# A searched program order, copies split by item, and a first token mix in halves, in a fused chunk-attention and wave-MLP kernel

## Chip, cores, metric

One core of a Trainium2 chip. The metric is the device time of one execution in microseconds (us), the median of several; lower is better. The profiled span of an execution is shorter than the time counted for the same execution (226.9 against 228.72 before the change).

## The reference

Chunked attention (chunks of 64 tokens, 8 heads of 64), then a layer that mixes tokens and channels:

```python
scores = 1/8 * (q_c @ k_c^T);  attn = softmax(scores);  x = attn @ v_c      # per 64-token chunk
theta = x @ w_theta
y = w_tok_r @ (x*cos(theta)) + w_tok_i @ (x*sin(theta))                      # over 576 tokens
u = x + y
out = u + relu(u @ w_ch)
```

The batch of 8 is worked in 4 pairs. 576 tokens of two batches are 9 blocks of 128, in five groups g = 0..4 of 2, 2, 1, 2, 2 blocks; group 2 is the block shared by both batches ("mid"). So a name such as a1 of (2,0) means step a1, pair 2, group 0.

## The kernel before

The engines are PE (TensorE, the matmuls; transposes run on it too), DVE (VectorE), ACT (ScalarE) and POOL (GpSimd). PSUM is the memory that PE writes its results to. Each pair goes through small steps. All use PE and one of four PSUM buffers, which DVE or ACT empties:

```python
a1(p,g)  # 32 transposes of q, k; qT copied by DVE, kT by ACT
a2(p,g)  # scores, exp on ACT
a3(p,g,hg)  # attn @ v; reciprocal and product on DVE
a4(p,g)  # transpose x; copy xT by ACT.  For the mid group:
        nc.scalar.copy(out=xm, in_=psv)
        for bb in range(2):
            nc.gpsimd.tensor_copy(                       # POOL
                out=xT[:, :, bb * S + KT * P : (bb + 1) * S],
                in_=xm[:, :, bb * CH : bb * CH + CH],
            )
a5(p,g)  # theta; cos and sin on ACT;  z(p,g): x*cos, x*sin on DVE
y(p,bb,db)  # token mix, 18 matmuls; uT = ps_y + xT on DVE
w(p,j)   # u @ w_ch and u; relu on ACT, sum and store (st)
```

The order comes from a small planner that weaves the attention of the next pair between the token mixes of this one. Loads cast f32 to f16 and are issued by POOL, the whole next pair at once:

```python
    for p in range(NP):
        ...                                    # first half of pair p, a4 of its mid group in it
        if more:
            new_pair(p + 1)
            load_batch(p + 1, B0 + B1)         # five groups: q, k, v
        ...                                    # second half, with a1, a2 of pair p+1 woven in
```

The softmax here doesn't subtract the row's maximum and nothing guards it: scores larger than these inputs give would overflow.

## Time and profile before

| | before |
|---|---|
| median time, us | 231.42 (229.97 to 231.69, 4 runs) |
| profiled span, us | 226.9 |
| PE busy | 89% |
| ACT, DVE busy | 58%, 53% |

Where a row of 40 digits is shown, it cuts the span into 40 equal slices, and each digit is the busy share of one slice in tenths. In a timeline a line has the start, the length, the engine, the source line, the operation, out<-in, the shape, and in brackets how long the engine had been idle and what ended it. The page's chain that ended last, by engine:

```profile
PE 75%; ACT 14%; DVE 6%; DMA 2%; issue 1%; POOL 0%; DVEq 0%; ACTq 0%; POOLq 0%
```

Three quarters of it are PE, so the way to less time is to fill PE's gaps. The view of stretches (start:end, length, then busy us of PE, PEld (weight loads), DVE, ACT, POOL; then the granted clock of PE, the DMA share and GB/s) shows how much there is:

```profile
110.00:170.00 60.00, 56.52 (x966) 40.46 (x961) 33.52 (x60) 39.99 (x45) 21.16 (x28) 1.00 0.84 104
170.00:222.00 52.00, 50.37 (x510) 33.41 (x508) 30.09 (x51) 24.19 (x33) 1.50 (x2) 1.00 0.20 64
```

PE lacks 3.5 us in 60 and 1.6 in 52: some 5 us in 112.

### The profile page before, as it was taken

The numbers are of one execution on the slowest core, as the hardware profiler recorded it, in microseconds if no ns is written. First come the engines' busy times: TensorE is split into PE (matmuls) and PEld (weight loads), VectorE is DVE, ScalarE is ACT, GpSimd is POOL, SyncE is SP. The second block draws the span as 40 slices with busy tenths as digits, with TensorE's granted clock in tenths as the row PEclk, the third lists the DMA queues.
The fourth block names the chain that finished last, engine by engine and source line by source line (L and its number), as shares of the span: only waits on it lengthen the run. The fifth ranks groups of instructions, "written<-read, shape, count | busy, mean of one in ns | idle before, by whom it ended". The sixth has DMA issues, their size and how long they took to land.

```text
span 226.9 us, 6743 instructions
## 1 busy us (share of the span) xinstructions
PE 201.7 (89%) x2994; PEld 140.3 (62%) x2994; DVE 120.2 (53%) x214; ACT 130.5 (58%) x151; POOL 88.5 (39%) x124
## 2 busy tenths in 40 slices
PE   0678979997898998999898998999898998999992
PEld 0564567855676656766785656666785657667751
DVE  0135373825547478446446477446456477356353
ACT  2355968357885881167785880267785880364142
POOL 8995487499100195981000295971000200000000
PEclk9999999999999999999999999999999999999998
DMA  6999999999920179999400189999200124013036
GB/s 63 165 156 186 192 180 187 144 124 168 222 22 3 48 102 197 221 168 208 129 3 3 49 118 225 195 169 222 99 3 3 49 69 139 3 46 139 2 110 217
DMA packets 83581, 26.93 MB, mean 119 GB/s; under 512 B 76256, under 2 KB 78944, under 8 KB 83552
## 3 DMA queue, kind: packets, MB, share of 16 engines
q0 software_dynamic: 77664, 16.54, 82.3%
q1 hardware_dynamic: 5888, 9.96, 12.6%
q8 instruction: 23, 0.38, 0.7%
q14 instruction: 6, 0.05, 0.1%
HBM read 33.06 MB, written 9.44 MB: 187 GB/s over the span
## 4 chain that ended last, share of the span: by engine, by line
PE 75%; ACT 14%; DVE 6%; DMA 2%; issue 1%; POOL 0%; DVEq 0%; ACTq 0%; POOLq 0%
PE ps_y L476 32%; PE ps_uw L496 13%; PE ps_theta L420 13%; ACT eT L342 5%; PE ps_qkT L307 5%; PE ps_sT L335 3%; PE ps_uw L503 3%; DMA qk<-in_k_dram 2%; PE ps_xT L391 2%; DVE uT L484 2%; DVE x L377 2%; ACT kT L317 2%; ACT cos L430 2%; ACT xT L398 2%; PE ps_x L363 2%
## 5 line engine op out<-in xcount | busy, mean ns | idle before, releaser
L476 PE MATMUL ps_y<-wT,z 128*128 128x288 f16 x512 | 68.2, 286 | 4.5 <-DVE x L377 2.4
L476 PEld LDWEIGHTS <-z 128*128 128x128 f16 x512 | 48.6, 98 | 18.5 <-DVE x L377 2.7
L246 POOL DMA_DIRECT2D v<-in_v_dram x56 | 42.1, 776 | 14.6 <-DMA qk<-in_k_dram 9.2
L484 DVE TENSOR_TENSOR uT<-ps_y,xT 128x576 f16<-128x576 f32 x32 | 24.2, 758 | 40.0 <-PE ps_y L476 40.0
L496 PE MATMUL ps_uw<-wch,uT 128*128 128x512 f16 x144 | 41.0, 379 | 2.3 <-ACT xT L398 1.7
L317 ACT COPY kT<-ps_qkT 128x1024 f16<-128x1024 f16 (+1 forms) x20 | 23.4, 1193 | 17.9 <-DVE qT L316 17.9
L404 POOL COPY xT<-xTm 128x256 f16<-128x256 f16 x8 | 4.9, 652 | 72.3 <-ACT xTm L402 72.3
L420 PE MATMUL ps_theta<-wtheta,xT 128*128 128x512 f16 x128 | 31.2, 388 | 1.7 <-ACT xT L398 1.7
L430 ACT ACTIVATE cos<-ps_theta,pihalf 128x1024 f16<-128x1024 f32 (+1 forms) x20 | 20.6, 1030 | 19.8 <-PE ps_theta L420 19.8
L503 PE MATMUL ps_uw<-id,uT 128*128 128x128 f16 x144 | 31.5, 219 | 0.0
L509 ACT ACTIVATE relu<-ps_uw 128x512 f32<-128x512 f32 x36 | 20.8, 603 | 18.4 <-PE ps_uw L503 18.4
L398 ACT COPY xT<-ps_xT 128x1024 f16<-128x1024 f16 x16 | 16.2, 1012 | 23.0 <-PE ps_xT L391 23.0
L515 DVE TENSOR_TENSOR o<-ps_uw,relu 128x512 f32<-128x512 f32 x36 | 24.0, 687 | 7.3 <-ACT relu L509 7.3
L307 PE MATMUL ps_qkT<-id,qk 128*64 128x128 f16 (+1 forms) x640 | 22.1, 227 | 6.4 <-DMA qk<-in_q_dram 5.8
L377 DVE TENSOR_TENSOR x<-ps_x,recip 128x512 f16<-128x512 f32 x36 | 24.9, 692 | 1.2
L307 PEld LDWEIGHTS <-qk 128*64 128x64 f16 (+1 forms) x640 | 18.9, 118 | 9.4 <-DMA qk<-in_q_dram 6.2
L316 DVE COPY qT<-ps_qkT 128x1024 f16<-128x1024 f16 (+1 forms) x20 | 12.6, 636 | 22.7 <-PE ps_qkT L307 22.7
L496 PEld LDWEIGHTS <-uT 128*128 128x128 f16 x144 | 14.1, 98 | 15.8
L420 PEld LDWEIGHTS <-xT 128*128 128x128 f16 x128 | 12.6, 100 | 15.7 <-ACT xT L398 2.1
L342 ACT ACTIVATE eT<-ps_sT 128x1024 f16<-128x1024 f32 (+1 forms) x20 | 18.3, 939 | 7.1 <-PE ps_sT L335 7.0
L443 DVE TENSOR_TENSOR z<-x,cos 128x1024 f16<-128x1024 f16 x16 | 11.1, 691 | 20.6 <-ACT cos L430 20.4
L225 POOL DMA_DIRECT2D qk<-in_k_dram x24 | 19.2, 804 | 3.6 <-DMA wch<-in_moe_w_ch_dram 1.6
(41 smaller groups left out, 199.1 us busy)
## 6 DMA issues: line engine op xcount, KB each, us to landing
out_dram<-o SPq DMA_DIRECT2D x32, 256.0 KB, 3.9
qk<-in_q_dram POOLq DMA_DIRECT2D x16, 256.0 KB, 6.4
qk<-in_k_dram POOLq DMA_DIRECT2D x16, 256.0 KB, 7.4
v<-in_v_dram POOLq DMA_DIRECT2D x40, 64.0 KB, 6.7
v<-in_v_dram POOLq DMA_DIRECT2D x16, 128.0 KB, 6.6
out_dram<-o SPq DMA_DIRECT2D x8, 128.0 KB, 4.1
wnat<-in_moe_w_tok_r_dram POOLq DMA_DIRECT2D x1, 576.0 KB, 9.9
wnat<-in_moe_w_tok_i_dram POOLq DMA_DIRECT2D x1, 576.0 KB, 11.9
```

The lines of the kernel that those rows point to most:

```text
L246: nc.gpsimd.dma_start(v16[pp : pp + m, sl, :, 0:D], v[2 * p + bb, :, s0 : s0 + m, :].rearrange("h s d -> s h d"),)
L307: nc.tensor.transpose(psv[par * D : par * D + D, w, e, tk, 0:rows], t[0:rows, w, 2 * e + par, tk, :], id16[0:rows, 0:rows],)
L317: nc.scalar.copy(out=kT[:, :, 0:rows, :].rearrange("p e s t -> p e t s"), in_=psv[:, 1, :, :, 0:rows],)
L342: nc.scalar.activation(out=eT[:, 0:n].rearrange("p i e r c -> p r (i e) c"), in_=psv[:, :, 0:n].rearrange("p r i e c -> p r (i e) c"), fun ...
L377: nc.vector.tensor_tensor(out=xo, in0=px[:, :, :, 0:D], in1=recip.broadcast_to((P, 2, NE, D)), op=ALU.mult,)
L420: nc.tensor.matmul(ps[:, jj * DM : jj * DM + DM], xt[:, db, :], wtheta16[:, db, :], start=(db == 0), stop=(db == NDB - 1),)
L430: nc.scalar.activation(out=cos[:, 0:n].rearrange("p a e -> p (a e)"), in_=pin, func=AF.Sin, bias=pihalf, scale=1.0,)
L476: nc.tensor.matmul(psv[:, hf, 0:HS], z[:, db * P : db * P + P], wT[:, kt, hf * HS : hf * HS + HS], start=(kt == 0), stop=(kt == 2 * KT),)
L484: nc.vector.tensor_tensor(out=s["uT"][:, db, sl].rearrange("p (f c) -> p f c", f=2), in0=psv[:, :, 0:HS], in1=s["xT"][:, db, sl].rearrange ...
L496: nc.tensor.matmul(ps[:, 0:DM], uT[:, db, j * P : j * P + P], wch16[:, db, :], start=(db == 0), stop=(db == NDB - 1),)
L503: nc.tensor.matmul(ps[:, DM + db * P : DM + db * P + P], uT[:, db, j * P : j * P + P], id16,)
L515: nc.vector.tensor_tensor(out=o, in0=ps[:, DM : 2 * DM], in1=r, op=ALU.add)
```

## The change

Its intent: replace the planner by a fixed list of items, found by annealing on a model of the engines; let each item say which engine makes its copies (the digit after the colon); begin the first token mix of pair 0 when half of the token weights are there. Loads run up to seven groups ahead, and each is issued as soon as the item that frees its buffer stands in the list. The core of the diff, cut:

```diff
+ORDER = """
+a1.0.0:3 a1.0.1:2 a2.0.0:0 a1.0.2:1 a3.0.0.0:0 a3.0.0.1:0 a2.0.1:0 a3.0.1.0:0 a2.0.2:0
+a3.0.2.0:0 a4.0.0:0 a4.0.2:1 ...
+... tw.1.1:1 yh.0.0:0 a1.0.3:3 yh.0.1:0 a2.0.3:0 a1.0.4:2 yh.1.0:0 a2.0.4:0 a3.0.3.0:0
+a1.1.2:3 yh.1.1:0 a2.1.2:0 a3.0.4.0:0 a1.2.0:0 a3.0.3.1:0 a1.1.0:0 a3.0.4.1:0 a2.2.0:0
+w.0.0:0 ...
-        nc.vector.tensor_copy(out=qT[:, :, :, 0:rows], in_=psv[:, 0, :, :, 0:rows])
-        nc.scalar.copy(out=kT..., in_=psv[:, 1, :, :, 0:rows])
+        copy(not bits & 1, qT[:, :, :, 0:rows], psv[:, 0, :, :, 0:rows])   # true: DVE, else ACT
+        copy(bits & 2, kT..., psv[:, 1, :, :, 0:rows])
...
+    LOADS = [(p, g) for p in range(NP) for g in BATCH[0] + BATCH[1]]
...                                        # the first seven loads up front, then:
+    for item in ORDER:
+        emit[kind](*args)
+        seen.add(name)
+        while loaded < len(LOADS):
+            p, g = LOADS[loaded]
+            pn, gn = LOADS[loaded - NAT]               # NAT = 7
+            need = {f"a1.{pn}.{gn}"}
+            if p >= 2:
+                need |= {f"a3.{p - 2}.{g}.{hg}" for hg in range(GROUPS[g][1])}
+            if not need <= seen:
+                break
+            load(loaded)
+            loaded += 1
```

## The prediction

> **What bounds the kernel now.** I read the page first (engine shares, the 40 slices, the issues of loads), then the timelines of PE, POOL, DVE and ACT over the first 70 us, then the waits.
>
> Engine shares and slices of the page:
> ```profile
> PE 201.7 (89%) x2994; PEld 140.3 (62%) x2994; DVE 120.2 (53%) x214; ACT 130.5 (58%) x151; POOL 88.5 (39%) x124
> ...
> POOL 8995487499100195981000295971000200000000
> ...
> DMA  6999999999920179999400189999200124013036
> ```
> PE is the bound: 89% busy, no other engine above 58%. POOL computes next to nothing; it is busy because it issues the loads of q, k, v. For the first eleven slices (62 us) it is near full and the DMA row is full: the weights and the first two pairs of batches stream in.
>
> The POOL timeline:
> ```profile
> 31.81 0.76 POOL L258 DMA_DIRECT2D wch<-in_moe_w_ch_dram  x1
> 32.56 0.75 POOL L404 COPY xT<-xTm 128x256 f16<-128x256 f16 x2
> 33.24 0.89 POOL L225 DMA_DIRECT2D qk<-in_q_dram  x1
> ...
> 54.82 1.47 POOL L246 DMA_DIRECT2D v<-in_v_dram  x2
> 56.48 0.89 POOL L246 DMA_DIRECT2D v<-in_v_dram  x1 [0.18 <-issue]
> 78.73 1.20 POOL L404 COPY xT<-xTm 128x256 f16<-128x256 f16 x2 [21.37 <-ACT xTm L402]
> ```
> POOL works strictly in order. At 31.81 it issues w_ch, at 32.56 it makes the two small copies xT<-xTm of pair 0, from 33.24 to 57.37 it issues the 25 loads of pair 1, and then it stands at the next copy for 21.37 us although loads stand behind it. So 25 issues take 24.1 us here: some 0.58 to 0.97 us each, plus about 5 us in which an issue waited for an earlier DMA.
>
> The issues of the page:
> ```profile
> qk<-in_q_dram POOLq DMA_DIRECT2D x16, 256.0 KB, 6.4
> qk<-in_k_dram POOLq DMA_DIRECT2D x16, 256.0 KB, 7.4
> ```
> A q or k load lands 6.4 and 7.4 us (median) after its issue.
>
> The DVE timeline, the first sum uT of pair 0:
> ```profile
> 35.98 0.76 DVE L484 TENSOR_TENSOR uT<-ps_y,xT 128x576 f16<-128x576 f32 x1 [1.68 <-PE ps_y L476]
> ```
> It reads xT, the middle columns that POOL copies included. The copy ended at 33.3, so this sum waited for PE alone. This is the place to remember.
>
> The waits of PE after 66 us sum to only 6.3 us in the trace, and PE is without a gap from 190 to 222. What a better order can win lies there and in the start.
>
> **What the Trainium skill says.** (1) "Perfetto Trace Analysis", section "DMA Instruction — SWDGE (GPSIMD)": the end shown for such a DMA is the end of descriptor generation, not of the transfer. The trace agrees: 0.6 to 1.0 us on POOL against 6.4 to 7.4 us to landing. (2) "ScalarE: Activation LUTs", "What ACT_TABLE_LOAD costs": about 1283 ns a load. The trace has 1283 ns, ten times. (3) "VectorE: DVE Perf Modes", the perf-mode tier table: a copy that reads PSUM runs at 2x at most. The trace agrees as far as it goes: the 1024-element copy qT takes 0.69 us on DVE, and xT, of the same size, 1.01 us on ACT. (4) "TensorE: Matmul & The Clock Gate", "What's actually happening": after an idle window PE starts at half clock. The trace shows it in
> ```profile
> 21.38 2.85 PE L420 MATMUL ps_theta<-wtheta,xT 128*128 128x512 f16 x8
> 24.94 1.89 PE L420 MATMUL ps_theta<-wtheta,xT 128*128 128x512 f16 x8
> ```
> where the same eight theta matmuls take 2.85 us early and 1.89 us later; the slices' clock row shows nothing of it.
>
> **The change part by part.** PE's work is the same: 5990 PE instructions in both built programs. I price each item by the length of its stretch in the PE timeline, without waits: a1 (32 transposes) 1.02 us, 0.66 for the half-size group; a2 0.63 and 0.35; a3 0.26; a4 0.45 and 0.22; a5 0.865 a token block; y 2.22; w 1.09; wT transposes 3 in all. With 36 w, 32 y and so on this gives 192.3 us. (PE's 201.7 is larger because each stretch also counts its draining tail.) Against 226.9 us there are 34.6 us to win: 5.8 before q lands, about 4.3 after the last matmul, 12.6 in the start up to 33.5 us (where 15.1 of the 192.3 are done), 2.4 from there to 66 (45.2 done), and about 9 after it.
>
> *Copies by item.* DVE takes 11 of the 20 xT copies (11 x about 0.95 leaves ACT, 11 x about 0.6 comes to DVE); qT and kT are exchanged in part (9 kT to DVE, 11 qT to ACT), about even. Two of ten table loads go: 2.6 us. ACT becomes about 117 us, DVE about 128. Neither bounds, so this counts only as smaller gaps.
>
> *First token mix in halves.* Four items of 18 matmuls, 256 or 320 columns wide in place of 288: same PE time. It could begin before the second half of the token weights is there. In the order, though, all six wT items stand before it, so it wins one or two us of the start at most.
>
> *New order and early loads.* Here I part with the intent. The loads now run seven groups ahead, issued as soon as a1 of an older group stands in the program. a1 of groups (0,0), (0,1), (0,2) are the first items, so loads (1,2), (1,3), (1,4) go into POOL's stream before the copy xT<-xTm of pair 0. The built program says so: that copy is POOL row 67, after all loads of pair 1; the kernel before has it ahead of all of these. POOL therefore reaches it only after the 25 issues that ended at 57.4 us, less the 0.7 us that the copy took ahead of them: about **57 us**, done about 58.3. The DVE instruction for the third half-mix (yh.1.0) waits for that copy, and DVE is in order. PE reaches yh.1.0 at about 38 us. With four PSUM buffers PE can run three items further, to about 43, and stands until 59.
>
> Next, the order puts a1 of group (2,0) seventh after yh.1.0, ahead of every w. Its load is POOL's next after the copy: q issued by 59.2, k by 60.1, and landing 6 us later, as the DMA still has pair 1 to finish (it fell idle at 63 in the kernel before): about 65.5. PE ends this a1 at **66.5 us**. By then it has done 28.8 us of its 192.3; the kernel before had done the 45.2. **The stall puts it 16.4 us behind.**
>
> What is left: 192.3 - 28.8 = 163.5 us, so the last matmul can't end before 230.0. Add 1.5 us for the half clock after the long pause (the theta line above lost 0.96 in one group), 5 us of gaps (before had about 9 in 147; I give the annealing half of it), and 4.3 for the last relu, sum and store. The span becomes 66.5 + 163.5 + 1.5 + 5 + 4.3 = **240.8 us**. The timed runs lie 3.1 to 4.8 us above the profiled span before; I add 3.7: **244.5 us**.
>
> Later loads hold nothing up by the same arithmetic: (2,1) is issued by 66.5 and used near 77, (3,1) issued by 90 and used near 105; POOL's copy for pair 1 falls near 93 and its first y sum near 107.
>
> **The rivals.** *The order works as meant.* If loads of (2,0) and the copy came by 45 us, PE would end near 192.3 + 5.8 + 4.3 plus 10 of gaps, 212 us of span, 216 timed, 7% faster. For it: PE's work is unchanged and gaps are to be had; an order found on a calibrated model should respect arrivals. Against it: POOL's stream before 57 us is full from end to end, and the same 9.4 MB precede this load in both kernels. *The stall is there but short.* If POOL issues faster (0.75 us each with no waits for DMAs, copy at 52) and the load lands in 4.5 us, PE passes at 60; with 3 us of gaps the span is 60 + 163.5 + 1.5 + 3 + 4.3 = 232.3 and the time 236: within 2%. For it: the shortest landing in the trace is 3.4 us. Against it: DMA is full in these slices. *ACT or DVE bind after the stall.* Between a1 of (2,0) and the next theta, 14 us of PE work carry about 11 us of ACT and 12 of DVE; with four PSUM buffers gaps could be 10 us rather than 5: 250 us.
>
> **Range and chances.** The copy's time is good to 1.5 us, landing to 2, gaps to 4: together 5 us at one in ten. Range 236.5 to 251. Faster by over 2% needs the whole stall to be absent: 0.04. Within 2% needs 8 us less: 0.09. Slower: 0.87.
>
> **What would show it.** In the new profile: POOL's copy xT<-xTm near 57 us with issues just ahead; a DVE wait of over 12 us for POOL at the half-mix sum; PE slices near zero from about 43 to 66 us, the last of it ended by DMA of k; PE busy nearly whole after it; eight table loads; ACT near 117 and DVE near 128. If the copy comes before 45 us, or PE has no gap over 5 us between 40 and 66, the argument is wrong.

## The result

| | before | after |
|---|---|---|
| median time, us | 231.42 | 246.12 (244.7 to 247.11, 4 runs) |
| ratio of fast runs | 1 | 1.0644 (95%: 1.0571 to 1.0717) |
| profiled span, us | 226.9 | 242.7 |

The kernel became 6.4% slower. A ratio here is the mean time of one kernel's fast runs over that of the other's in the same rounds, so it is not quite the ratio of the medians quoted. Executions over 1.5% slower than the fastest of the same kernel are left out of the means.

The page after, shares and slices:

```profile
PE 203.8 (84%) x2994; PEld 142.0 (58%) x2994; DVE 128.4 (53%) x223; ACT 117.3 (48%) x137; POOL 88.8 (37%) x126
...
PE   0849996063298999958999999999999999999992
...
POOL 8994686799779777940000200000010000000000
PEclk9999999557579999997999999999999999999998
DMA  7999999999999999993104021201321212221236
```

PE has a hole in slices 7 to 11, at 40 to 67 us. The clock row falls to 5 with it. DMA is full up to the eighteenth slice; loads now stream without a break. The chain that ended last:

```profile
PE 66%; DMA 16%; POOL 9%; issue 3%; DVE 2%; ACT 2%; ACTq 0%; POOLq 0%
```

DMA was 2% of it and POOL 0%; now they are 16% and 9%. POOL's timeline:

```profile
55.14 2.32 POOL L177 DMA_DIRECT2D v<-in_v_dram  x3
57.37 0.83 POOL L362 COPY xT<-xTm 128x256 f16<-128x256 f16 x2
58.05 0.96 POOL L156 DMA_DIRECT2D qk<-in_q_dram  x1
58.92 0.96 POOL L156 DMA_DIRECT2D qk<-in_k_dram  x1
...
97.09 0.76 POOL L362 COPY xT<-xTm 128x256 f16<-128x256 f16 x2
```

The mid copy of pair 0 stands at 57.37, after all loads of pair 1, and q and k of (2,0) follow it. In the kernel before it stood at 32.56. DVE:

```profile
37.81 1.30 DVE L198 COPY kT<-ps_qkT 128x1024 f16<-128x1024 f16 x1
57.90 0.82 DVE L443 TENSOR_TENSOR uT<-ps_y,xT 128x640 f16<-128x640 f32 x1 [18.78 <-POOL xT L362]
```

Between these two lines DVE did nothing for 18.78 us: the half-mix sum reads the columns that POOL copies. PE over the hole:

```profile
37.10 1.26 PE L435 MATMUL ps_y<-wT,z 128*128 128x320 f16 x8
...
40.16 0.30 PE L321 MATMUL ps_x<-v,eT 64*64 64x65 f16 x16
50.41 1.37 PE L267 MATMUL ps_qkT<-id,qk 64*64 64x64 f16 x32 [9.95 <-DMA qk<-in_q_dram]
51.72 2.31 PE L435 MATMUL ps_y<-wT,z 128*128 128x320 f16 x8
...
60.25 0.46 PE L293 MATMUL ps_sT<-qT,kT 64*64 64x64 f16 x16 [3.66 <-DVE kT L198]
...
63.76 1.06 PE L267 MATMUL ps_qkT<-id,qk 128*64 128x128 f16 x16 [2.83 <-DMA qk<-in_q_dram]
66.81 1.06 PE L267 MATMUL ps_qkT<-id,qk 128*64 128x128 f16 x16 [1.99 <-DMA qk<-in_k_dram]
```

Three waits lie in a row: 9.95 us for q of group (1,2), 3.66 for DVE's copy kT, which stood behind the wait for POOL, and 2.83 + 1.99 for q and k of (2,0). After them the order does what it was made for (stretches, as above):

```profile
70.00:110.00 40.00, 34.81 (x797) 24.91 (x798) 28.83 (x52) 30.38 (x32) 30.29 (x41) 1.00 1.79 166
110.00:170.00 60.00, 60.00 (x931) 42.57 (x932) 35.99 (x64) 34.16 (x42) 1.50 (x2) 0.97 0.14 44
170.00:230.00 60.00, 60.00 (x509) 40.02 (x507) 33.21 (x55) 26.33 (x35) 0.75 (x2) 1.00 0.22 73
```

From 110 us PE is busy 120 us of 120, where the kernel before lost 5 of 112. So the search did fill the gaps; the hole ahead of them cost more.

### The profile page after: what moved, and what is told of

It reads as the page before. It is cut to its first block, busy times and chain, and to the rows that moved or that the text cites. A ratio compares the mean times of both kernels' runs of the same rounds, so it can differ in the third digit from the quotient of the medians.

```text
span 242.7 us, 6736 instructions
## 1 busy us (share of the span) xinstructions
PE 203.8 (84%) x2994; PEld 142.0 (58%) x2994; DVE 128.4 (53%) x223; ACT 117.3 (48%) x137; POOL 88.8 (37%) x126
## 4 chain that ended last, share of the span: by engine, by line
PE 66%; DMA 16%; POOL 9%; issue 3%; DVE 2%; ACT 2%; ACTq 0%; POOLq 0%
PE ps_y L456 26%; DMA qk<-in_k_dram 12%; PE ps_uw L476 12%; PE ps_theta L378 11%; PE ps_qkT L267 5%; POOL v L177 4%; DMA wnat<-in_moe_w_tok_r_dram 4%; POOL qk L156 3%; PE ps_uw L483 3%; PE ps_xT L349 3%; PE ps_sT L293 3%; PE ps_x L321 2%; ACT kT L200 1%; DVE qT L198 1%; DVE o L495 1%
## 5 line engine op out<-in xcount | busy, mean ns | idle before, releaser
L456 PE MATMUL ps_y<-wT,z 128*128 128x288 f16 x448 | 60.7, 290 | 0.0
L456 PEld LDWEIGHTS <-z 128*128 128x128 f16 x448 | 42.8, 99 | 13.2
L267 PE MATMUL ps_qkT<-id,qk 128*64 128x128 f16 (+1 forms) x640 | 24.7, 238 | 21.8 <-DMA qk<-in_q_dram 18.9
L476 PE MATMUL ps_uw<-wch,uT 128*128 128x512 f16 x144 | 42.5, 379 | 0.2 <-ACT kT L200 0.2
L464 DVE TENSOR_TENSOR uT<-ps_y,xT 128x576 f16<-128x576 f32 x28 | 21.2, 756 | 32.4 <-PE ps_y L456 32.2
L267 PEld LDWEIGHTS <-qk 128*64 128x64 f16 (+1 forms) x640 | 20.8, 125 | 24.5 <-DMA qk<-in_q_dram 19.6
L156 POOL DMA_DIRECT2D qk<-in_q_dram x24 | 19.4, 811 | 1.0 <-POOLq L559 0.8
L200 ACT COPY qT<-ps_qkT 128x1024 f16<-128x1024 f16 (+1 forms) x11 | 9.5, 859 | 20.6 <-PE ps_qkT L267 20.5
L200 ACT COPY kT<-ps_qkT 128x1024 f16<-128x1024 f16 (+1 forms) x11 | 13.3, 1212 | 11.7 <-DVE qT L198 11.7
L392 ACT ACTIVATE sin<-ps_theta 128x1024 f16<-128x1024 f32 (+1 forms) x20 | 18.7, 937 | 0.0
```

The lines of the kernel that those rows point to most:

```text
L156: nc.gpsimd.dma_start(t[(pp // 2) : (pp // 2) + m // 2, ti].rearrange("p h t d -> p h (t d)"), src.rearrange("h (p t) d -> p h (t d)", t=2),)
L200: nc.scalar.copy(out=out, in_=in_)
L267: nc.tensor.transpose(psv[par * D : par * D + D, w, e, tk, 0:rows], t[0:rows, w, 2 * e + par, tk, :], id16[0:rows, 0:rows],)
L456: nc.tensor.matmul(psv[:, hf, 0:HS], zt[:, db * P : db * P + P], wT[:, kt, hf * HS : hf * HS + HS], start=(kt == 0), stop=(kt == 2 * KT),)
L464: nc.vector.tensor_tensor(out=uT_tile(p)[:, db, sl].rearrange("p (f c) -> p f c", f=2), in0=psv[:, :, 0:HS], in1=xT_tile(p)[:, db, sl].rea ...
L476: nc.tensor.matmul(ps[:, 0:DM], uT[:, db, j * P : j * P + P], wch16[:, db, :], start=(db == 0), stop=(db == NDB - 1),)
```

## The experiments

Twelve kernels ran. The question was which of the two late arrivals made the hole, POOL's copy or the loads, and whether the order and the split are good once they are fed. The first four ran on one chip, the next four on another; each is compared with the kernel before. Kernels are compared only within the same rounds.

### 1. The mid copy on DVE

```diff
-            nc.gpsimd.tensor_copy(
+            nc.vector.tensor_copy(
```

> Edit: in the changed kernel the two small copies xT<-xTm go to DVE instead of POOL; order and loads stay. Main theory (two late arrivals in series: POOL's copy, and the loads of groups (1,2) and (2,0) which the order uses before they land): DVE's 18.8 us wait for POOL is gone, but PE still waits near 40 for q of (1,2) until about 50 and for k of (2,0) until about 66; time 244 to 247 us, the same as the changed kernel. Rival A (the copy behind the loads is the cause): the stall is gone, 228 to 231 us. Rival B (the new order or the new split of copies is slow by itself): 246 us, with PE gaps elsewhere.

Measured 244.48 us, ratio 1.058 (1.0523 to 1.0637). PE's timeline:

```profile
50.67 1.34 PE L267 MATMUL ps_qkT<-id,qk 64*64 64x64 f16 x32 [9.77 <-DMA qk<-in_q_dram]
...
64.51 1.06 PE L267 MATMUL ps_qkT<-id,qk 128*64 128x128 f16 x16 [7.01 <-DMA qk<-in_q_dram]
66.20 1.06 PE L267 MATMUL ps_qkT<-id,qk 128*64 128x128 f16 x16 [0.63 <-DMA qk<-in_k_dram]
```

The wait for POOL is gone and the time is not: PE waits for the same two groups until nearly the same moments (50.67 and 66.20, against 50.41 and 66.81). Rival A falls: the copy by itself is not worth 15 us.

### 2. The copy on DVE, the early items later

```diff
-a2.0.4:0 a3.0.3.0:0 a1.1.2:3 yh.1.1:0 a2.1.2:0 a3.0.4.0:0 a1.2.0:0 a3.0.3.1:0 a1.1.0:0 a3.0.4.1:0 a2.2.0:0
+a2.0.4:0 a3.0.3.0:0 yh.1.1:0 a3.0.4.0:0 a3.0.3.1:0 a1.1.0:0 a3.0.4.1:0
...                                    # a1, a2 of (1,2) now ahead of a3 of (1,2); a1, a2 of (2,0)
...                                    # and a1 of (2,1) ahead of w.0.2
```

> Edit: the copy on DVE, and in the order a1 and a2 of (1,2) stand later (just ahead of a3 of (1,2)), a1 and a2 of (2,0) and a1 of (2,1) later still (ahead of the third w of pair 0). Main theory: PE no longer waits for (2,0); pair-1 groups (1,3) and (1,1) land near 50 to 55 and PE waits for them some 5 to 10 us at about 47; time about 236 us, 8 to 12 under the changed kernel. Rival A: 228 to 231. Rival B: 243 to 247, no gain beyond the copy.

Measured 236.15 us, ratio 1.0236 (1.0163 to 1.0309). What is left of the hole:

```profile
54.09 1.06 PE L265 MATMUL ps_qkT<-id,qk 128*64 128x128 f16 x16 [5.41 <-DMA qk<-in_q_dram]
```

With the copy on DVE already, a few moved items gave back 8.3 us of experiment 1's time; its verdict against the kernel before, at a limit of 2%, is unclear. In this part PE now waits for a load only here, 5.41 us for q of (1,3) and then 0.65 for its k, and its other waits are under 2 us.

### 3. The early items later, the copy still on POOL

The order of experiment 2, with POOL's copy:

```diff
-a1.1.2:3 yh.1.1:0 a2.1.2:0 a3.0.4.0:0 a1.2.0:0 ...
+yh.1.1:0 a3.0.4.0:0 ...                # the same items moved as in experiment 2, nothing else
```

> Edit: only the order of the changed kernel is altered, as in the run with the copy on DVE and the early items later; the copy stays on POOL. Main theory (the two late arrivals are alternative causes of the same stall): POOL's copy at 57 us alone holds DVE for 15 us or more and PE stands from about 43 to 59; 243 to 249 us, as slow as the changed kernel, so that each fix alone is worth next to nothing and both together gave 10 us. Rival (early use of loads is the one cause): 236 us as with both.

Measured 245.99 us, ratio 1.0618 (1.0551 to 1.0685). POOL's and PE's timelines:

```profile
57.16 0.83 POOL L360 COPY xT<-xTm 128x256 f16<-128x256 f16 x2
```

```profile
58.57 0.44 PE L319 MATMUL ps_x<-v,eT 64*64 64x65 f16 x16 [15.29 <-DVE uT L441]
```

PE waits for no load here, and 15.29 us for the sum on DVE that waits for POOL. With experiments 1 and 2 this fills a table of medians:

| | items early | items later |
|---|---|---|
| copy on POOL | 246.1, ratio 1.064 (the change) | 246.0, ratio 1.062 |
| copy on DVE | 244.5, ratio 1.058 | 236.2, ratio 1.024 |

Each fix alone gives under 2 us, both give 10 (the ratios are the fair comparison). The two causes stand in parallel over the same 27 us: whichever is left alone still holds PE.

### 4. The old order with POOL's copy, and with DVE's

The frame of the changed kernel (loads ahead, weights in two parts) with the order and the copies of the kernel before; then also the copy on DVE.

```diff
-ORDER = (the searched list)
+ORDER = (the list that the planner of the kernel before emits, old engine for every copy, whole y)
-    BATCH = [[0, 1, 2], [3, 4]]
+    BATCH = [[0, 2, 1], [3, 4]]
```

> Edit: the changed kernel's frame (loads ahead by seven groups, halves of the token weights in two parts) with the program order and the assignment of copies of the kernel before, whole y items; POOL keeps the copy. Main theory: nothing of pair 1 is used early, but POOL reaches the copy only at about 57 us, behind the loads of pair 1, and DVE stands at the first y sum from about 36; time 246 to 253 us, as slow as the changed kernel or slower, with the old order. Rival B (the new order is the cause): 229 to 233 us, as the kernel before.

Measured 252.76 us, ratio 1.0948 (1.0895 to 1.1001). Its waits (total, times, longest):

```profile
DVE uT L462 <- POOL xT L360: 23.5, 1, 23.5
```

So the slowdown comes without the new order: it is enough to let the loads pass ahead of POOL's copy.

> Edit: as the run with the old order, but the two small copies on DVE. Main theory: the 23.5 us wait of DVE for POOL was the whole loss there, and nothing of pair 1 is used before it lands; time back to 228 to 231 us, about 22 under the run with POOL's copy and level with the kernel before or a little faster. Rival (loads that run seven groups ahead disturb by themselves, through DMA or POOL): 236 us or more.

Measured 232.73 us, ratio 1.0046 (0.9994 to 1.0097). The whole loss was that one wait. In this order, loads that run ahead neither help nor hurt beyond the noise.

### 5. Loads in the order of use

```diff
-            nc.gpsimd.tensor_copy(
+            nc.vector.tensor_copy(
-    LOADS = [(p, g) for p in range(NP) for g in BATCH[0] + BATCH[1]]
+    LOADS = [tuple(...) for item in ORDER if item.startswith("a1.")]
```

> Edit: the copy on DVE, and the loads are issued in the order in which the a1 items use them ((1,2), (2,0), (1,0), (1,3), ... after pair 0); the order of the computing is that of the changed kernel. Main theory: (1,2) lands near 42, (2,0) near 46, the later groups still come only every 4 us; the stall of 27 us shrinks to some 10 us in pieces; time about 233 to 236 us. Rival A: 228 to 231, as in the first run. Rival B: 243 to 247.

This build was faulty: 252.41 us and a wrong result. (2,0) became one of the first seven loads, which are issued without asking, and its v went over that of pair 0. PE's timeline shows a wait of 31.93 us for v at its very first a3. The time says nothing on the theories. Mended, so that this load too waits for a3 of (0,0):

> Edit: as the run with the loads in the order of use, with its fault mended: load (2,0) overwrote v of pair 0 before it was read, since the first seven loads were issued without asking for that; now it waits for a3 of (0,0). Copy on DVE, order of the computing as in the changed kernel. Main theory: the 10 us wait for (1,2) falls to 2 to 4, the wait for (2,0) is gone, waits of about 5 us each for later groups ((1,0), (1,1)) take their place as the loads still come at one group in 4 us; 231 to 237 us. Rival (the order or the split is slow by itself): 243 to 247. Result correct.

The mend, cut:

```diff
-    for i in range(5, NAT):
-        load(i)
-    loaded = NAT
+    loaded = 5                             # only five groups up front; (1,2) and (2,0) come in the loop
...
-            need = {f"a1.{pn}.{gn}"}
+            need = set()
+            if loaded >= NAT:
+                pn, gn = LOADS[loaded - NAT]
+                need = {f"a1.{pn}.{gn}"}
```

Measured 230.93 us, ratio 0.9958 (0.9919 to 0.9997), and correct. Two of its waits:

```profile
48.16 0.64 PE L267 MATMUL ps_qkT<-id,qk 128*64 128x128 f16 x16 [1.65 <-DMA qk<-in_q_dram]
...
58.16 0.64 PE L267 MATMUL ps_qkT<-id,qk 128*64 128x128 f16 x16 [2.25 <-DMA qk<-in_q_dram]
```

The order of computing is that of the changed kernel, item for item, and 15 us are gone. What remains between 40 and 62 us are waits for loads of 0.8 to 2.3 us each; the order still wants the loads a little sooner than they come. (There is also a pause of 4.11 us at 91.4 that no release in the trace ends.) The rival that the order or the split is slow by itself falls.

### 6. Whole first mixes for halves

The kernel of experiment 2 with whole items at the same four places:

```diff
-yh.0.0:0 ... yh.0.1:0 ... yh.1.0:0 ... yh.1.1:0
+y.0.0.0:0 ... y.0.0.1:0 ... y.0.0.2:0 ... y.0.0.3:0
```

> Edit: as the run with the copy on DVE and the early items later, but the first token mix of pair 0 in four whole y items in place of four halves, at the same places. Main theory: all transposes of the token weights stand ahead of the first mix in either form, so the halves give nothing: 235 to 238 us, within 1% of that run. Rival (the halves shorten the start or ease DVE): 239 us or more.

Its four runs were 234.73, 235.69, 240.13 and 240.16 us; the last two count as slow, so that two fast ones are left. These two, and the profiled span of 233.9 us, lie at those of experiment 2 (four runs from 235.39 to 238.45, span 234.3). The trace shows the first mix 1.7 us later (31.95 against 30.22): half of it because w_theta landed later in this execution, half a wait of 0.93 us for the last copy wT, which experiment 2 doesn't have there. Of this delay 0.6 us is left after the wait for q of (1,3), at 54.67 against 54.09. As far as two fast runs and a trace show, the halves give nothing that lasts in this order; in an order without that wait they were not tried.

### 7. A search with the true arrivals

I searched again for an order, with the copy on DVE, on a model in which loads arrive as the traces show (a group about every 4 to 5 us, (2,0) near 65 us). Its list takes (1,0) and (1,1) first and leaves (2,0) until after 60:

```diff
+a1.0.3:2 y.0.0.1:0 y.0.0.2:0 a2.0.3:0 a1.0.4:0 y.0.0.3:0 a3.0.3.0:0 a3.0.3.1:0 a2.0.4:0 y.0.0.0:0
+a1.1.0:0 a3.0.4.1:0 a3.0.4.0:0 w.0.1:0 a2.1.0:0 st.0.1:0 a4.0.4:0 a4.0.3:0 a3.1.0.0:0 a1.1.1:0 ...
```

> Edit: a new program order, found by the same kind of search, but with the arrivals of the loads as the trace shows them (one group in about 4 to 5 us, (2,0) near 65) and the copy on DVE; copies split between DVE and ACT by item as the search chose; whole first y items. Main theory: PE waits less than 10 us in all after the start, span about 217 to 221 and time 219 to 225 us, 3 to 5% faster than the kernel before. Rival (a searched order can't hold on the chip, gaps from engines come back): 228 us or more.

Measured 222.97 us, ratio 0.9626 (0.9586 to 0.9665): faster than both kernels. Stretches:

```profile
50.00:110.00 60.00, 57.85 (x1171) 41.02 (x1168) 40.32 (x74) 46.81 (x49) 46.67 (x62) 1.00 1.85 170
110.00:170.00 60.00, 60.00 (x787) 40.33 (x785) 38.73 (x71) 34.76 (x38) 0.00 (x0) 1.00 0.14 42
```

PE is busy 117.9 us of these 120, against 112.0 in the kernel before (55.5 and 56.5 in the same stretches).

Then the same list with the digits that choose the engine set back:

```diff
-(a1 and a4 items with the digit that the search chose)
+(every a1 and a4 item with digit 0: qT on DVE, kT and xT on ACT)
```

> Edit: the order searched with the true arrivals, but every copy on the engine that it had in the kernel before (qT on DVE, kT and xT on ACT). Theory 1 (the split by item matters once the order is tight): ACT near 131 us, gaps from ACT come back, 226 to 231 us, 4 to 8 more than with the split. Theory 2 (the split is worth nothing, the order does it all): 222 to 225.

Measured 228.5 us, ratio 0.9861 (0.9821 to 0.9902). The same stretches:

```profile
50.00:110.00 60.00, 55.66 (x1101) 38.93 (x1102) 34.07 (x67) 49.36 (x52) 46.79 (x62) 1.00 1.84 168
110.00:170.00 60.00, 58.75 (x827) 40.05 (x823) 34.23 (x64) 38.72 (x43) 0.00 (x0) 1.00 0.13 43
```

With every copy on its old engine ACT is busy 49.4 us of the first 60 in place of 46.8 and DVE 34.1 in place of 40.3, and PE loses 3.4 us of the 120, of 5.5 us by which the time rose. Theory 1 holds.

And the old order, copy on DVE, with the searched digits:

```diff
-(every a1 and a4 item with digit 0)
+(every a1 and a4 item with the digit that it has in the searched list)
```

> Edit: the order of the kernel before with the copy on DVE (232.7 us as measured), and every q, k and xT copy on the engine that the searched order gave it. It fills the fourth cell of order by split. If the split is worth its 5.5 us by itself, 226 to 228 us; if it pays only with an order that it was chosen for, 230 to 235 us, since in the old order PE's gaps come from the sequence of exp, sin and first y, and not from the load of ACT. I expect the second.

Measured 232.33 us, ratio 1.0016 (0.9962 to 1.007). The four cells, as ratios to the kernel before, the copy on DVE in all:

| | old split | searched split |
|---|---|---|
| old order | 1.0046 | 1.0016 |
| order searched with arrivals | 0.9861 | 0.9626 |

The order alone gives 1.8%, the split alone 0.3% (inside the noise), both 4.2%. The split pays only in the order that it was searched with.

The last kernel exchanges the first two items of the searched list:

```diff
-a1.0.1:3 a1.0.0:3 a1.0.2:2 a2.0.1:0 a2.0.0:0 ...
+a1.0.0:3 a1.0.1:3 a1.0.2:2 a2.0.0:0 a2.0.1:0 ...
```

> Edit: the searched order with its first two a1 items (and their a2) exchanged, so that PE starts with group (0,0), which lands first; the profile of the searched order shows PE starting at 8.6 us in place of 5.8. Theory: the start gains 1 to 2.5 us, 220 to 222 us. Rival (v of the first group or ACT sets the start anyway): 222 to 224, no change.

Measured 222.34 us, ratio 0.9564 (0.95 to 0.9627). One of four runs, the profiled one, counts as slow. The interval overlaps that of the list before the exchange, so whether the exchange gains is not settled.

## Why the prediction was right

The time was forecast at 244.5 us and came at 246.12; the span at 240.8 and came at 242.7. By its steps:

- **POOL's copy.** Forecast at 57 us, done at 58.3; it was at 57.37 and done at 58.20. The wait of DVE for it, "over 12 us", was 18.78.
- **The load of (2,0).** PE was to leave its a1 at 66.5; it did at 66.81 + 1.06 = 67.9, since k landed 1.3 us later than I said.
- **The rest.** From there to the last matmul, near 238.4, are 170.5 us. If the work is the forecast's 163.5, 7.0 remain for pauses and a slow clock, for which it had 6.5. The tail was 4.3. PE's waits in this stretch sum to 5.2 us, but not the gaps that I meant: 4.0 of them have no release that the trace shows, 3.48 of these at 106.5. The half clock explains about the remaining 1.8, in two places that cost 0.8 and 1.4 us. Right after the hole 32 transposes took 1.85 us in place of 1.01 (granted clock 0.50 from 68 to 70 us); after the pause at 106.5 the mix at 110.14 took 3.67 in place of 2.31 (0.50 from 111 to 114). Inside the hole it cost nothing: the half-mix at 51.72 took 4.86 us at a granted clock of 0.50 to 0.55, the one at 37.10 took 2.62 at 1.00, and PE had to wait until 60.25 in any case.
- **From span to time.** I added 3.7 us, which mixed two things: the same execution is counted 1.8 us longer than its span before and 2.0 after, and each profiled execution was faster than the median of the timed runs, by 2.7 and 1.4 us. That both together were alike (4.5 and 3.4) is luck.
- **Loads that come later** held nothing up, as said; the copy of pair 1 was at 97.09, 4 us later than said, still ahead of its use, the sum that ran at 119.28 and not near 107.
- **Engines.** ACT 117.3 and DVE 128.4 us busy and eight table loads, all as forecast.

Some things were off. I let PE run to about 43 us and then stand for POOL; in truth it stopped at 40.5, for a load of pair 1 that I had not checked, (1,2), and worked again from 50.41 to 56.6, where I had said that its slices would be near zero. All this lay inside the same hole, so the sum stood, by luck. I gave the halves "one or two us" of the start and the order nothing; the first mix began at 29.82 in place of 33.50, 3.7 us sooner, of which experiment 6 leaves at most 1.7 to the halves, and the hole took that too.

Some readings were wrong without weight in the sum. POOL issues 26 loads for pair 1 and not 25 (the timeline's counts), and its waits for DMAs among them are 3.6 us and not 5. POOL's row is not near full for eleven slices: four of these are at 4 to 7 tenths and the eleventh at 1; it is the DMA row that is full. And the theta line at 21.38 doesn't show a clock that fell after an idle window: the longest wait of PE from 17 us to there is 0.51 us, and the granted clock reads 1.00 in the stretch. The slower pace there, 2.85 us against 1.89, stays unexplained; the half clock after a long wait is seen only after the change, in the lines above.

The text treated copy and load as one chain, one after the other: the copy's stall to 59, then the load to 66.5. The experiments show them as two bars across the same road: taking either away gives under 2 us.

The rival "works as meant" failed because the order used groups before they landed and the copy stood behind the loads. The full stream of loads, the reason given against it, is only part of that: in experiment 5 as many loads stream, in the order of use, and 15 us are gone. It was right about what an order can do: from 110 us on, with its loads there, this one leaves PE without a gap, and another list, searched with the true arrivals, makes the kernel 3.7% faster.

## What to carry to other kernels

An order found on a model is as good as the model's times of arrival: put the queue of loads in it, with its rate and its order, before the engines. When loads are issued ahead, look at what small work shares the issuing engine, since that work moves behind all of them. And if removing one suspected cause changes nothing, remove a second with it before giving either up.

## What the Trainium skill lacked or had wrong

- "VectorE: DVE Perf Modes": the tier table gives a copy from PSUM up to 2x; the section "What auto-detection actually checks" asks for a step of one in every tensor. The runs agree and give the price: DVE makes the 128x1024 copy qT in 0.69 us and kT, which writes every second element, in 1.30 us, the same as ACT's 1.31. So moving kT to DVE buys balance and no speed. The table alone would mislead here; the two sections together don't.
- "TensorE: Matmul & The Clock Gate", "Part 4: PE-mode transpose", says that the full clock does not engage for transposes. Here 16 transposes of a1 took 1.06 us at 66.81, right after the hole (66 ns each, granted clock 0.50), and 32 took 1.08 us at 72.83 (34 ns each, granted clock 1.00), between other matmuls: they run at the granted clock. Whether transposes alone would bring the full clock, no run shows.
- No page that I read puts a size on pauses of PE without a wait: 3.48 us in the middle of sixteen equal small matmuls at 106.5 us after the change, 4.11 us in the mended run of experiment 5, and 1.6 to 2.7 us in experiments 1 to 4.

```profile
109.95 0.25 PE L321 MATMUL ps_x<-v,eT 64*64 64x65 f16 x7 [3.48 <-issue]
```

What these pauses are, no run settles. A late load of PE's own instructions would fit: in both of the longer pauses the DMA queue that the profile calls "instruction" moves one packet of 0.02 MB (within 107 to 108 us, and within 93 to 94 us). But such packets also pass where PE doesn't pause, and nothing was tried.
